# Top-k mask of an attention kernel: one parametric relu on ScalarE in place of a relu and a GpSimd subtraction

## The chip, the cores and the metric

The kernel runs on one core of a Trainium2 chip. The metric is the device time of one execution in microseconds (us); lower is better. The engines are named as in the profile: PE is TensorE's matmul (PEld its weight load), DVE is VectorE, ACT is ScalarE, POOL is GpSimd, SP is SyncE, which issues nearly all DMAs.

## The reference

Attention over 4 batches and 8 heads, 576 positions and 64 columns per head. Of each row of scores only the 32 largest stay, and the softmax runs over these. Two expert layers of 2304 x 512 x 2048 follow.

```python
scores = scale * np.matmul(q, k.transpose(0, 1, 3, 2))        # scale = 1 / 8
kth = np.partition(scores, -top_k, axis=-1)[..., -top_k:-top_k + 1]   # top_k = 32
scores = np.where(scores >= kth, scores, -1000000000.0)
attn = np.exp(scores - np.max(scores, axis=-1, keepdims=True))
attn = attn / (np.sum(attn, axis=-1, keepdims=True) + 1e-09)
x = np.matmul(attn, v)                       # then [tokens, 512]
h = np.maximum(x @ w_in, 0.0);  x = h * h @ w_out             # first layer
h = x @ w_in;  out = np.maximum(0.01 * h, h) @ w_out          # second layer
```

## The kernel before

The work of attention goes in 144 tiles of 128 rows of scores (128 x 576, fp32), two to a pair, 72 pairs. Products are exact to fp32 by splitting each operand into a high and a low part, which is why so many subtractions stand in the code.

**Scores** (L279, L280): TensorE writes a tile in two halves of 288, and ScalarE copies them into a score buffer `s` (six buffers, `NS`). The tiles of two batches are computed early, stored to HBM and loaded again when they are due (L283, L287).

**Top-k** (L834, L836): VectorE finds the 32 largest of each row in four rounds of MAX8 with a MATCH_REPLACE8 between them, so seven instructions a tile. They go into `m8`: element 0 is the row's maximum, element 31 the 32nd largest.

**Mask and exponential.** For each pair GpSimd makes two shifts by one product (`shifts`, L291): nb = -0.125 x maximum, kf = 2^100 x 32nd largest. For each tile, `drop` has ScalarE compute relu(kf - 2^100 s) (L298), which is 0 for scores that stay and huge for the others, and GpSimd subtract that from the score (L299). `expo_sum` (L303) takes exp(0.125 e + nb) on ScalarE and sums the row. GpSimd adds 1e-9 to the pair's sums (L307) and VectorE takes the reciprocal `rc` (L308). The tile `e` has four buffers.

**Behind it** TensorE transposes e (L317, L330), ScalarE copies it out (L325, or L322 with VectorE's low part L323 for later units), TensorE multiplies with V (L401, or L412). In the first units the reciprocals are transposed as well (L351), copied to `rb` (L366) and multiplied in by VectorE (`xn`, L432), and ScalarE makes the high part `xh` (L433).

**Expert blocks.** Once 512, 256, 384, ... rows of x are complete, a block of that size runs both layers, 16 steps each: twelve products into `h` (L580), an activation on ScalarE and GpSimd, and products into `acc` (L623, L625). The first block reads the weights raw (L490), converts them with ScalarE and VectorE (L513 to L519), splits them on ScalarE (L523) and GpSimd (L526), and SyncE stores the result (L534, L535); later blocks load it. A step's split may stand on GpSimd only behind the latest subtraction of `drop`: that is what `behind("pool")` asks for, with the key that L299 sets.

**Order.** The code places all of this in a grid of slots, 16 to a pair (first relu at slot 14, exponentials at 16 and 17, reciprocal at 18). A scheduler then writes for each engine one fixed order, from priorities and from its own estimate of how long things take. On the chip each engine takes its instructions in that order and waits at the first whose inputs are not there.

Of the kernel before, what the change touches and what calls it, by code (L numbers as in the profile page):

```python
# [8 lines left out]
F = mybir.dt.float32  # L9
R = mybir.dt.float32r  # L10
U = mybir.dt.uint32
AF = mybir.ActivationFunctionType
OP = mybir.AluOpType
# [3 lines left out]
FAR = 2.0 ** 100  # L17
# [54 lines left out]
def topk_attention_moe_moe2_kernel(  # L72
# [12 lines left out]
    P = 128  # L85
# [8 lines left out]
    PE, ACT, DVE, POOL, SP = nc.tensor, nc.scalar, nc.vector, nc.gpsimd, nc.sync  # L94

    const = ctx.enter_context(tc.tile_pool(name="const", bufs=1))
    pool = ctx.enter_context(tc.tile_pool(name="work", bufs=2))
# [3 lines left out]
    def bank():  # L101
        return psum.tile([P, 512], F, tag="att", name="att", bufs=3)

    ident = const.tile([P, P], F, tag="ident", name="ident")
    make_identity(nc, ident)
    scales = const.tile([P, 2, 2], F, tag="scales", name="scales")
    POOL.memset(scales[:, :, 0], -0.125)
    POOL.memset(scales[:, :, 1], FAR)

    def behind(key):  # L110

        return tc.issue_after(cur[key].ins) if key in cur else ExitStack()
# [48 lines left out]
    for i in range(4):  # L161
        x = const if i < 2 else ahead
# [124 lines left out]
        SP.dma_start(t["s"], t["sd"])  # L287

    def shifts(pr):
        t = pool.tile([P, 2, 2], F, tag="kf", name="kf", bufs=2)  # L290
        POOL.tensor_tensor(t, pr["m8"][:, :, 0:32:31], scales, op=OP.mult)  # L291
        pr["nb"], pr["kf"] = t[:, :, 0], t[:, :, 1]

    def drop(pr, i):
        t = pr["t"][i]
        t["e"] = ebufs[t["i"] % NE]
        e, x = t["e"], t["s"]
        ACT.activation(e, x, AF.Relu, bias=pr["kf"][:, i:i + 1], scale=-FAR)  # L298
        cur["pool"] = POOL.tensor_tensor(e, x, e, op=OP.subtract)  # L299

    def expo_sum(pr, i):
        e = pr["t"][i]["e"]
        ACT.activation(e, e, AF.Exp, bias=pr["nb"][:, i:i + 1], scale=0.125,  # L303
                       accum_out=pr["sum"][:, i:i + 1])

    def recip(pr):
# [68 lines left out]
    cur = dict(fill=0, rate=0.0)  # L375
# [99 lines left out]
    def w_alloc(i):  # L475
        wi = pool.tile([P, 2, 512], R, tag="wi", name="wi", bufs=3)
        wo = pool.tile([P, 2, 512], R, tag="wo", name="wo", bufs=4)
        wt[i] = (wi, wo)
        return wi, wo
# [16 lines left out]
    def w_convert(i):  # L496
        g = w_convert_steps(i)
        while True:
            with tc.high_priority(offset=CONVP):
                if next(g, 1):  # L500
                    return
            yield

    def w_convert_steps(i):
        if i >= len(steps) or not fresh[i]:
            return
        w2 = w_alloc(i)
        for raw, w in zip(wraw.pop(i), w2):
            if W64:
                lo, hi = raw[:, :, 0], raw[:, :, 1]  # L510
                b = pool.tile([P, 512], U, tag="wc", name="wc", bufs=WCB)
                v = bank()
                ACT.activation(b, lo, AF.Copy, scale=L_SCALE, bias=L_BIAS)  # L513
                ACT.activation(v, hi.bitcast(F), AF.Copy, scale=H_SCALE)  # L514
                yield 0
                vu, c = v.bitcast(U), b.bitcast(F)
                with behind("dve"):
                    DVE.scalar_tensor_tensor(b, vu, 3, b, op0=OP.logical_shift_left, op1=OP.bitwise_or)
                DVE.scalar_tensor_tensor(b, vu, 0x80000000, b, op0=OP.bitwise_and, op1=OP.bitwise_or)  # L519
                yield 0  # L520
            else:
                c = raw
            ACT.activation(w[:, 0, :], c, AF.Copy)  # L523
            yield 0
            with behind("pool"):
                POOL.tensor_tensor(w[:, 1, :], c, w.bitcast(F)[:, 0, :], op=OP.subtract)  # L526
            yield 0

    def w_store(i):
# [129 lines left out]
    for uh in uhs:  # L659
        b, hp, i = uh["b"], uh["hp"], uh.get("di")  # L660
# [79 lines left out]
    for p in range(NPAIRS):  # L740
        pr = dict(t=tiles[2 * p:2 * p + 2], p=p)
        pairs.append(pr)
        z = 16 * p
        for i, t in enumerate(pr["t"]):
            if direct(t["uh"]):
                at(z - DLEAD + 5 * i, scores, t, 0)
                at(z - DLEAD + 2 + 5 * i, scores, t, 1)
            else:
                at(z - LEAD + i, load_s, t)
            if i == 0:  # L750
                at(z + 14, shifts, pr)
            at(z + 14 + i, drop, pr, i)
            at(z + 16 + i, expo_sum, pr, i)
            if split(t["uh"]):
                at(z + 20 + i, norm, pr, i)
            at(max(z + 20 + 3 * i, z + 21 + i), pt_main, t)
        at(z + 18, recip, pr)
        at(z + 26, pt_left, pr)
# [60 lines left out]
    while slot <= last:  # L819
        p, i = divmod(slot, 16)  # L820
        if slot >= 0 and p < NPAIRS:
            pr = pairs[p]
# [6 lines left out]
            x = i % 2  # L829
            t = pr["t"][x]  # L830
            m8 = pr["m8"]
# [78 lines left out]
```

## Time and profile before

| | |
|---|---|
| three runs | 1211.27, 1215.92, 1216.74 us; median 1215.92 |
| profiled execution, span | 1212.2 us (first to last instruction; its time as a run is not one of the three) |
| PE / PEld busy | 1139.7 us (94%) / 994.3 us (82%) |
| DVE busy | 945.4 us (78%) |
| ACT busy | 877.0 us (72%) |
| POOL busy | 791.0 us (65%) |

The table is an average over stages with different limits, and an instruction's busy time overlaps the start of the next, so two instructions in a row take a little less than twice the mean. "Idle before" in a group of instructions is time in which the engine stood still just before them, with what ended it. The chain of waits follows the end of the execution back, at each step to what released it.

### The profile page before, as it was taken

The page shows a single profiled execution, that of the slowest core. Times are in us where ns is not written, and L with a number is a line of the kernel's source. Part 1 is how long each engine was busy: PE and PEld are TensorE (multiplying, and loading weights), DVE is VectorE, ACT ScalarE, POOL GpSimd, SP SyncE. Part 2 cuts the span into 40 slices and gives each one's busy share as a digit, 9 for nine tenths or more (in the row PEclk, how much of TensorE's full clock was granted, in tenths as well). Part 3 has the DMA queues.
Part 4 walks back from the last instruction along what each step waited for, and adds up shares of the span by engine and source line. Part 5 has one row for each costly group of instructions (what it writes and reads, how often), then busy time and mean ns, then how long its engine had stood idle before and what let it go on. Part 6 is the DMA issues. An engine that isn't in the chain of part 4 may idle for free.

```text
span 1212.2 us, 20368 instructions
## 1 busy us (share of the span) xinstructions
PE 1139.7 (94%) x6388; PEld 994.3 (82%) x6388; DVE 945.4 (78%) x1944; ACT 877.0 (72%) x1939; POOL 791.0 (65%) x948
## 2 busy tenths in 40 slices
PE   5898878998899999999999999999999999999998
PEld 4676766886677879988998898788788899999997
DVE  7999999668888899999999999999999910110122
ACT  6889899888899997877767777676777763334322
POOL 7998977877889886667777685666576754004300
PEclk9899997999999999999999999999999999999999
DMA  9665656879889888889988788667576579779974
GB/s 308 230 226 194 196 196 245 268 252 315 306 292 343 296 279 272 301 289 367 349 294 286 256 280 285 202 229 233 193 232 223 197 261 374 255 254 339 359 251 137
DMA packets 110521, 323.24 MB, mean 267 GB/s; under 512 B 17488, under 2 KB 25680, under 8 KB 110416
## 3 DMA queue, kind: packets, MB, share of 16 engines
q1 hardware_dynamic: 107776, 317.24, 77.1%
q10 hardware_dynamic: 2640, 4.72, 1.1%
q8 instruction: 51, 0.84, 0.3%
q14 instruction: 54, 0.44, 0.1%
HBM read 254.54 MB, written 67.37 MB: 266 GB/s over the span
## 4 chain that ended last, share of the span: by engine, by line
PE 67%; ACT 10%; DVE 9%; DMA 3%; issue 2%; POOL 1%; ACTq 0%; SPq 0%; POOLq 0%
PE h L580 28%; PE acc L623 14%; PE acc L625 13%; DVE m L834 4%; PE att L412 3%; DVE w L836 3%; PE att L317 3%; DMA wraw<-in_w_dram 2%; PE att L401 2%; ACT e L303 2%; PE att L279 1%; ACT att L514 1%; ACT stage L280 1%; DVE PTs L323 1%; ACT s L280 1%
## 5 line engine op out<-in xcount | busy, mean ns | idle before, releaser
L580 PE MATMUL h<-xh,wi 128*128 128x512 f32 (+2 forms) x1280 | 350.0, 345 | 9.1 <-ACT wi L523 3.9
L834 DVE MAX8 m<-w 128x8 f32<-128x576 f32 x432 | 312.7, 748 | 1.5
L580 PEld LDWEIGHTS h<-xh,wi 128*128 128x128 f32 x1280 | 226.8, 190 | 38.6 <-ACT wi L523 4.3
L299 POOL TENSOR_TENSOR e<-s,e 128x576 f32<-128x576 f32 x144 | 203.4, 1431 | 26.6 <-ACT e L298 25.4
L836 DVE MATCH_REPLACE8 w<-m,w 128x576 f32<-128x576 f32 x288 | 213.2, 743 | 0.5
L580 PE MATMUL h<-xl,wi 128*128 128x512 f32 (+2 forms) x640 | 206.5, 340 | 1.4 <-DVE xl L637 1.1
L606 POOL TENSOR_TENSOR gl<-ga,gh 128x512 fp32r<-128x512 f32 (+2 forms) x160 | 162.8, 1017 | 38.1 <-ACT gh L605 32.5
L623 PE MATMUL acc<-gh,wo 128*128 128x512 f32 (+2 forms) x768 | 155.1, 340 | 0.0
L625 PE MATMUL acc<-wo,gh 128*128 128x512 f32 x576 | 151.5, 398 | 3.0 <-ACT gh L605 3.0
L603 POOL TENSOR_TENSOR ga<-ga,gb 128x512 f32<-128x512 f32 (+2 forms) x80 | 81.3, 1017 | 107.6 <-ACT gb L602 105.4
L623 PEld LDWEIGHTS acc<-gh,wo 128*128 128x128 f32 x768 | 125.9, 188 | 10.8 <-ACT gh L591 0.4
L580 PEld LDWEIGHTS h<-xl,wi 128*128 128x128 f32 x640 | 120.4, 189 | 14.7 <-DVE xl L637 4.0
L303 ACT ACTIVATE e<-e,kf 128x576 f32<-128x576 f32 x144 | 112.5, 782 | 17.3 <-POOL e L299 17.0
L625 PEld LDWEIGHTS acc<-wo,gh 128*128 128x128 f32 x576 | 103.9, 188 | 23.2 <-ACT gh L605 4.7
L298 ACT ACTIVATE e<-s,kf 128x576 f32<-128x576 f32 x144 | 105.7, 778 | 22.4 <-POOL kf L291 20.3
L834 DVE MAX8 m<-s 128x8 f32<-128x576 f32 x144 | 104.7, 748 | 13.4 <-ACT s L280 12.4
L592 POOL TENSOR_TENSOR ga<-ga 128x512 f32<-128x512 f32 (+2 forms) x80 | 66.2, 828 | 68.2 <-ACT gh L591 66.0
L836 DVE MATCH_REPLACE8 w<-m,s 128x576 f32<-128x576 f32 x144 | 107.0, 743 | 0.6
L317 PE MATMUL att<-ident,e 128*128 128x128 f32 x576 | 89.4, 284 | 13.0 <-ACT e L303 7.5
L312 ACT ACTIVATE e<-e,rc 128x576 f32<-128x576 f32 x108 | 78.0, 773 | 21.3 <-DVE rc L308 21.1
L317 PEld LDWEIGHTS att<-ident,e 128*128 128x128 f32 x576 | 69.8, 145 | 26.6 <-ACT e L303 12.8
L623 PE MATMUL acc<-gl,wo 128*128 128x512 f32 (+2 forms) x384 | 86.7, 345 | 0.2 <-POOL gl L606 0.2
(96 smaller groups left out, 2174.4 us busy)
## 6 DMA issues: line engine op xcount, KB each, us to landing
wi<-wd SPq DMA_DIRECT2D x160, 512.0 KB, 5.1
wo<-wd SPq DMA_DIRECT2D x160, 512.0 KB, 5.3
wraw<-in_w_dram SPq DMA_DIRECT2D x64, 512.0 KB, 5.6
sd<-stage SPq DMA_DIRECT2D x72, 288.0 KB, 2.8
s<-sd SPq DMA_DIRECT2D x72, 288.0 KB, 4.8
wd<-wi SPq DMA_DIRECT2D x32, 512.0 KB, 6.0
wd<-wo SPq DMA_DIRECT2D x32, 512.0 KB, 6.2
kraw<-in_k_dram SPq DMA_DIRECT2D x16, 576.0 KB, 4.3
```

The source lines that it names most:

```text
L298: ACT.activation(e, x, AF.Relu, bias=pr["kf"][:, i:i + 1], scale=-FAR)
L299: cur["pool"] = POOL.tensor_tensor(e, x, e, op=OP.subtract)
L303: ACT.activation(e, e, AF.Exp, bias=pr["nb"][:, i:i + 1], scale=0.125, accum_out=pr["sum"][:, i:i + 1])
L312: ACT.activation(e, e, AF.Copy, scale=pr["rc"][:, i:i + 1])
L317: PE.transpose(ps[:, j * P:(j + 1) * P], t["e"][:, j * P:(j + 1) * P], ident)
L580: PE.matmul(h[:, 0:n], lhsT=wi[:, w, c * P:(c + 1) * P], rhs=x[c][y][:, 0:n], start=cnt == 0, stop=cnt == 3 * NK - 1)
L603: POOL.tensor_tensor(a[:, 0:n], a[:, 0:n], b[:, 0:n], op=OP.subtract)
L606: (DVE if j >= GLD else POOL).tensor_tensor(gl[:, 0:n], a[:, 0:n], gh.bitcast(F)[:, 0:n], op=OP.subtract)
L623: PE.matmul(acc[c][:, 0:n], lhsT=wo[:, w, cs], rhs=g[:, 0:n], start=first, stop=last)
L625: PE.matmul(acc[c], lhsT=g[:, cs], rhs=wo[:, w, :], start=first, stop=last)
L834: cur["dve"] = DVE.max(out=m8[:, x, 8 * r:8 * r + 8], in_=t["s"] if r == 0 else t["w"])
L836: cur["dve"] = DVE.match_replace(out=t["w"], in_to_replace=m8[:, x, 8 * r:8 * r + 8], in_values=t["s"] if r == 0 else t["w"], imm_value=NEG)
```

## The change

The relu and the subtraction of `drop` become one parametric relu on ScalarE: with x = 32nd largest - s, it passes x where x is positive (the score is to be dropped) and multiplies x by 0.125 x 2^-100 where it is not. The exponential then scales by -2^100: a dropped score gives exp of a huge negative number, 0, and a kept one exp(0.125 (s - 32nd largest) + nb). The shift nb is now 0.125 x (32nd largest - maximum), made by two GpSimd instructions, and kf is gone: the parametric relu reads the 32nd largest from `m8`. The constant tile `scales` goes, and the weights' split has no `behind("pool")` any more, since nothing sets that key.

```diff
@@ kernel
-    scales = const.tile([P, 2, 2], F, tag="scales", name="scales")
-    POOL.memset(scales[:, :, 0], -0.125)
-    POOL.memset(scales[:, :, 1], FAR)
@@ shifts, drop, expo_sum
     def shifts(pr):
-        t = pool.tile([P, 2, 2], F, tag="kf", name="kf", bufs=2)
-        POOL.tensor_tensor(t, pr["m8"][:, :, 0:32:31], scales, op=OP.mult)
-        pr["nb"], pr["kf"] = t[:, :, 0], t[:, :, 1]
+        t = pool.tile([P, 2], F, tag="nb", name="nb", bufs=2)
+        POOL.tensor_tensor(t, pr["m8"][:, :, 31], pr["m8"][:, :, 0], op=OP.subtract)
+        POOL.tensor_scalar(t, t, 0.125, 1.0, op0=OP.mult, op1=OP.mult)
+        pr["nb"] = t
 
     def drop(pr, i):
         t = pr["t"][i]
         t["e"] = ebufs[t["i"] % NE]
-        e, x = t["e"], t["s"]
-        ACT.activation(e, x, AF.Relu, bias=pr["kf"][:, i:i + 1], scale=-FAR)
-        cur["pool"] = POOL.tensor_tensor(e, x, e, op=OP.subtract)
+        ACT.activation(t["e"], t["s"], AF.Prelu, bias=pr["m8"][:, i, 31:32], scale=-1.0, alpha=0.125 / FAR)
 
     def expo_sum(pr, i):
         e = pr["t"][i]["e"]
-        ACT.activation(e, e, AF.Exp, bias=pr["nb"][:, i:i + 1], scale=0.125,
+        ACT.activation(e, e, AF.Exp, bias=pr["nb"][:, i:i + 1], scale=-FAR,
                        accum_out=pr["sum"][:, i:i + 1])
@@ w_convert_steps
-            with behind("pool"):
-                POOL.tensor_tensor(w[:, 1, :], c, w.bitcast(F)[:, 0, :], op=OP.subtract)
+            POOL.tensor_tensor(w[:, 1, :], c, w.bitcast(F)[:, 0, :], op=OP.subtract)
```

Lines behind `drop` are numbered 4 lower in the changed kernel, those behind `w_convert_steps` 5 lower. The instructions of TensorE, ScalarE, VectorE and SyncE are as many as before; GpSimd has 144 fewer subtractions, 72 more small ones and two fills less. But the scheduler wrote a new order for every engine. VectorE where the first block's last x is made (a number behind m names a pair's top-k: 2556 and 2842 before are two neighbouring pairs, as 2536 and 2821 are now; xn is the product that completes x, in L432 and L428), before:

```order
L834 MAX m_2556<-w 128x8
L836 MATCH_REPLACE w<-m_2842,w 128x576
L308 RECIPROCAL rc<-sum 128x2
L836 MATCH_REPLACE w<-m_2842,s_105 128x576
L834 MAX m_2842<-w 128x8 x2
L836 MATCH_REPLACE w<-m_2842,w 128x576
L432 TENSOR_TENSOR xn<-att,rb 128x256
```

The same place in the changed kernel:

```order
L304 RECIPROCAL rc<-sum 128x2
L831 MATCH_REPLACE w<-m_2536,w 128x576 x2
L829 MAX m_2536<-w 128x8 x2
L831 MATCH_REPLACE w<-m_2536,w 128x576
L428 TENSOR_TENSOR xn<-att,rb 128x256
L831 MATCH_REPLACE w<-m_2821,s_101 128x576
```

Before, xn stood in the middle of the second pair's rounds; now it stands ahead of the second pair's first replace, with a last MAX8 of the first pair still behind it. Counted from the start of the program, 149 MAX8 and 112 MATCH_REPLACE8 stood ahead of it, and 145 and 108 do now.

ScalarE at the same place (the masks and exponentials of the pair that is then under way; xh is the first block's last copy), before:

```order
L298 ACTIVATE e_112<-s_108,kf 128x576
L298 ACTIVATE e_113<-s_109,kf 128x576
L280 ACTIVATE s_106<-att 128x288
L366 ACTIVATE rb<-att 64x256
L514 ACTIVATE att<-wraw 128x512
L303 ACTIVATE e_112,sum<-e_112,kf 128x576
L280 ACTIVATE s_106<-att 128x288
L433 ACTIVATE xh_658<-xn 128x256
```

And in the changed kernel:

```order
L295 ACTIVATE e_109<-s_105,m_2536 128x576
L277 ACTIVATE s_103<-att 128x288
L429 ACTIVATE xh_652<-xn 128x256
L510 ACTIVATE att<-wraw 128x512
L321 ACTIVATE PT<-att 128x4x128
L510 ACTIVATE att<-wraw 128x512
L295 ACTIVATE e_110<-s_106,m_2536 128x576
L299 ACTIVATE e_109,sum<-e_109,nb 128x576
```

The second mask and the first exponential of that pair have moved from ahead of xh to behind it, and the masks read m directly.

VectorE at the 48th of the 72 reciprocals, in the stage of the later units, before:

```order
L340 TENSOR_TENSOR PTs<-att,PTs 64x256
L834 MAX m_8747<-w 128x8
L834 MAX m_8890<-w 128x8
L836 MATCH_REPLACE w<-m_8747,w 128x576
L308 RECIPROCAL rc<-sum 128x2
L836 MATCH_REPLACE w<-m_8890,w 128x576
L418 TENSOR_TENSOR xf<-att,tmp 64x256
```

And in the changed kernel, where m_8696 and m_8838 are the same two pairs:

```order
L336 TENSOR_TENSOR PTs<-att,PTs 64x256
L829 MAX m_8838<-s_103 128x8
L829 MAX m_8838<-s_104 128x8
L831 MATCH_REPLACE w<-m_8696,w 128x576
L829 MAX m_8696<-w 128x8
L304 RECIPROCAL rc<-sum 128x2
L829 MAX m_8696<-w 128x8
```

The reciprocal has moved ahead of rounds that it stood behind: 394 MAX8 of the program came before it, and 391 do now. Of eleven reciprocals looked at, each fourth from the 28th to the 68th, nine stand behind one to three MAX8 fewer than before, two behind as many.

## Rows read from the trace of the kernel before

**Rows 1.** Busy time of each engine in four stretches; columns as in the first line.

```profile
0.00:205.00 205.00, 163.20 (x851) 130.33 (x851) 193.71 (x413) 176.11 (x464) 175.53 (x247) 0.92 0.69 228
205.00:450.00 245.00, 232.68 (x1133) 188.75 (x1133) 202.24 (x382) 223.54 (x458) 208.60 (x208) 0.98 0.85 291
450.00:975.00 525.00, 512.26 (x2979) 455.55 (x2978) 514.73 (x1086) 392.80 (x827) 358.05 (x425) 1.00 0.78 263
975.00:1212.00 237.00, 231.52 (x1430) 219.70 (x1428) 34.74 (x66) 84.59 (x193) 48.85 (x69) 1.00 0.81 283
```

**Rows 2.** Chain of waits from 205 to 450 us, shares of that stretch.

```profile
by line: PE h L580 26.3%; PE acc L625 14.5%; DMA wraw<-in_w_dram 10.6%; PE acc L623 9.4%; PE att L401 4.0%; ACT att L514 4.0%; issue 3.3%; PE att L279 2.5%; ACT wc L513 2.4%; ACT e L303 2.2%; ACT wi L523 1.9%; ACT wo L523 1.7%; DMA wd<-wo 1
```

**Rows 3.** Groups of instructions, whole span: busy us, mean ns | idle before <-releasers.

```profile
L299 POOL TENSOR_TENSOR e<-s,e 128x576 f32<-128x576 f32 x144 | 203.4, 1431 | 26.6 <-ACT e L298 25.4 <-PE att L317 0.9
...
L303 ACT ACTIVATE e<-e,kf 128x576 f32<-128x576 f32 x144 | 112.5, 782 | 17.3 <-POOL e L299 17.0
...
L298 ACT ACTIVATE e<-s,kf 128x576 f32<-128x576 f32 x144 | 105.7, 778 | 22.4 <-POOL kf L291 20.3 <-PE att L330 1.0 <-issue 0.6
...
L291 POOL TENSOR_TENSOR kf<-m,scales 128x4 f32<-128x4 f32 x72 | 14.4, 200 | 26.7 <-DVE m L834 25.4
...
L308 DVE RECIPROCAL rc<-sum 128x2 f32<-128x2 f32 x72 | 11.1, 154 | 2.7 <-POOL sum L307 2.3
...
L116 ACT ACT_TABLE_LOAD x1 | 1.3, 1283 | 0.7 <-PEq L897 0.7
```

**Rows 4.** Pieces of the chain of waits, 185 to 206: start us, us, what.

```profile
194.16 0.99 POOL e L299
...
195.53 1.42 POOL e L299
196.95 1.23 POOL wi L526
198.18 1.25 POOL wo L526
...
200.46 0.20 POOL kf L291
...
200.69 1.44 ACT e L298 x2
...
202.45 0.38 ACT rb L366
...
205.04 1.22 PE h L580 x2
```

**Rows 5.** GpSimd's busy time in line L299 by stretch (the first number after the comma).

```profile
205.00:450.00 245.00, 28.42 (x20) 0.98 0.85 291
450.00:975.00 525.00, 123.91 (x88) 1.00 0.78 263
```

**Rows 6.** VectorE's later MAX8, from 100 to 200 and from 900 to 975 us.

```profile
L834 DVE MAX8 m<-w 128x8 f32<-128x576 f32 x57 | 40.6, 745 | 0.0
...
L834 DVE MAX8 m<-w 128x8 f32<-128x576 f32 x36 | 25.8, 746 | 0.1
```

**Rows 7.** VectorE's instructions in order of time around xn: start us, us.

```profile
201.32 1.41 DVE L834 MAX8 m<-w 128x8 f32<-128x576 f32 x2
202.65 0.07 DVE L836 MATCH_VALUE_LOAD w<-m,w 128x8 f32 x1
...
203.37 0.41 DVE L432 TENSOR_TENSOR xn<-att,rb 128x256 f32<-128x256 f32 x1
```

**Rows 8.** SyncE's queue waiting, 205 to 450 us: total us, times, longest.

```profile
SPq L490 <- ACT att L514: 83.9, 42, 8.1
SPq L534 <- POOL wi L526: 26.4, 19, 3.7
SPq L535 <- POOL wo L526: 25.5, 16, 4.7
```

**Rows 9.** VectorE waiting, 205 to 450 us, in the same columns.

```profile
DVE wc L518 <- ACT att L514: 24.2, 15, 3.6
```

## Prediction

> **What bounds the kernel now.** I read the span first in four stages [rows 1], cut where TensorE starts the first expert block (205), where VectorE's load changes (450) and where the top-k work ends (975). In each stage the reader is to see which engine has no room. Up to 205 it is VectorE: 193.7 of 205 us busy, the rest mostly start-up. From 450 to 975 it is VectorE again, 514.7 of 525, beside a TensorE that is almost as full (512.3). In the last stage only TensorE matters, 231.5 of 237. The stage from 205 to 450 is mixed: TensorE 232.7, ScalarE 223.5, GpSimd 208.6 and VectorE 202.2 of 245. Here the weights are read raw, split and stored, and the chain of waits carries 10.6% of this stage as landing time of raw weights [rows 2].
>
> So GpSimd, which the change relieves, is nowhere the fullest engine. Its subtraction costs 144 x 1.431 = 206 us when each is taken by itself, 203.4 as busy time [rows 3], and yet ScalarE waited for it only 17.0 us in all. What it is worth must be read from the chain. The chain of waits shows it on the path at one place that counts, just ahead of the first expert block [rows 4]: two subtractions of 0.99 and 1.42 us, behind them two weight splits (1.23 and 1.25), which by the code may not be issued before the subtraction, and then the shift kf, for which ScalarE's relus wait while the copy rb, on which the block hangs, is queued behind them.
>
> **The change part by part.** The sum is made against this execution's span, 1212.2 us; the median of the runs, 1215.9, is 3.7 above it, and I add that at the end.
>
> *The subtraction goes.* 144 x 1.43 us leave GpSimd: 28.4 of its load in the mixed stage (20 of them) and 123.9 from 450 to 975 [rows 5], the rest up to 205. From 450 to 975 this is hidden already: VectorE never stops there, and its top-k rounds don't wait for the masked scores. Worth there: 0.
>
> *Does VectorE run faster with a quieter GpSimd?* From 100 to 200 us a MAX8 took 745 ns, from 900 to 975, where GpSimd does much less, 746 [rows 6]; no effect, so 0. The Trainium skill (GPSIMD Engine Reference, Specifications) says that GpSimd shares its memory interface with VectorE and that they contend when a VectorE instruction has two SBUF inputs or runs in a two-port mode. By that rule the VectorE-bound stages could get shorter; by the rows the MAX8, more than half of the top-k work, does not feel it, and the sum stays.
>
> *The shift.* One product of 200 ns for kf and nb [rows 3] becomes two small instructions for nb. The second, on 128x2, has that 200 ns as its nearest row: 72 x 0.2 = 14.4 us more GpSimd time. It lies beside the two parametric relus of the pair (1.44 us for two relus now [rows 4]), since these no longer wait for the shift but for VectorE's last MAX8 itself. The cover is gone when GpSimd's queue is more than a microsecond late; then the exponential waits for nb as the relu waited for kf before (20.3 us in all [rows 3]), with ScalarE's copies queued behind.
>
> *Prelu for Relu.* The same 128x576 elements with one per-partition operand, on the same engine. Nearest rows: Relu 778, Exp 782 ns [rows 3]. I take 778, cost 0; at 782 it would be 0.6 us over all 144, so the ends are 0 and +0.6 and no gain. The table is another matter. The program of before loads one activation table, 1283 ns [rows 3]; in the changed ScalarE order there is still one load, at its head. The Trainium skill (ScalarE: Activation LUTs, Table sets) says that functions come in sets and that each switch costs about 2.7 us; by that, an Exp and a Prelu from different sets would be a loss of hundreds of microseconds. The order shows no switch, so the sum carries none.
>
> *The order around the first block (term A).* The product xn closes the last head pair of the first expert block; TensorE's block starts 1.7 us behind it (203.37 [rows 7], 205.04 [rows 4]). In the old VectorE order 149 MAX8 and 112 replaces stand ahead of it, in the new one 145 and 108: four rounds less. Two MAX8 take 201.32 to 202.65, one replace with its load 202.65 to 203.37 [rows 7], so this is 4 x 0.665 + 4 x 0.72 = 5.5 us of VectorE time. VectorE has been late for nothing there, so its order is its clock. ScalarE is the next that could be late: ahead of the same block's copy xh it has one relu and one exponential less, about 0.78 + 0.78 = 1.6 us [rows 3], plus its waits for GpSimd. The true gain lies between 1.6 and 5.5; I take 4.5, nearer to VectorE, because VectorE is the fuller of the two up to 205 (193.7 against 176.1 [rows 1]). The four rounds are not saved, only done later: in the mixed stage, where VectorE has 43 us free.
>
> *The mixed stage (term B).* SyncE stood 26.4 + 25.5 = 51.9 us waiting for GpSimd's weight splits before it could store them [rows 8], and the next raw loads are issued behind on the same queue. The splits may now go ahead of the softmax work, and 28.4 of GpSimd's 208.6 us are gone, 13.6%. If SyncE's waits shrink by as much, that is 7.1 us; but raw loads are only a tenth of this stage's chain, ScalarE is 91% busy with unchanged work and VectorE's longest wait is for ScalarE (24.2 us [rows 9]), not for GpSimd. Bounds 0 and 7; I take 2.5, a third. What is late next is ScalarE.
>
> *The rest.* The constant tile and its two fills go, at the start, beside the first loads: 0. Score buffers are released one GpSimd instruction earlier, so reloads of scores leave earlier on SyncE; no engine of the path waits for these: 0. The last stage is the same products in the same order: 0.
>
> Sum: 1212.2 - 4.5 - 2.5 = 1205.2, plus 3.7: **1209 us**.
>
> **The rivals.**
>
> *Rival 1, nothing arrives.* The scheduler wrote an order that assumes early softmax results; if ScalarE, not VectorE, sets the pace up to 205, A is only 1.6, and the mixed stage, which depends on ScalarE and on raw weights, gives it back. For it: ScalarE's load is unchanged, and GpSimd is on the chain almost nowhere else. Against it: xn came in its VectorE place without delay. It gives 1212 to 1219, about 1216.
>
> *Rival 2, more.* If the raw loads really hang on SyncE's waits for GpSimd, half of their 10.6% of 245 us on the chain may go: 13 us, with A in full 18.5: 1193.7 + 3.7, some 1197. For it: 51.9 us of SyncE waiting. Against it: before its raw loads it waits longest for ScalarE, 83.9 us [rows 8]. The port rule above would also come out near here; the MAX8 rows speak against it.
>
> *Rival 3, slower: the reciprocal blocks VectorE.* In the new order each reciprocal stands earlier among the top-k rounds. Of the 44 pairs after 450 us one has on average 1 to 2 MAX8 and as many replaces less ahead of it, some 2 us. VectorE takes its instructions in order, so when sum or nb is late, all top-k rounds behind the reciprocal stop, in the stage where VectorE is the bound. Now that costs 2.3 us over all 72 [rows 3]. At 0.5 us a pair it would be 44 x 0.5 = 22: 1212.2 - 4.5 + 22 + 3.7 = 1233. It decides from 0.1 us a pair (4.5 / 44). Against it: the chain from relu to exponential loses a subtraction of 1.43 us and more, about what the reciprocal was moved.
>
> *Rival 4, the table.* Should the functions need separate sets, even one load of 1.283 us a pair and back, 144 in all, is 185 us: about 1400. The order excludes it but for an error of mine.
>
> **How the numbers follow.** A measurement of this kernel can tell about 0.5%, so faster means below 1209.8 and slower above 1222.0. The forecast has 0.48, with its own range 1204 to 1214, of which 0.29 falls below 1209.8 and 0.19 within; rival 1 has 0.22, all within; rival 2 0.16, all faster; rival 3 0.12 and rival 4 0.02, slower. Together faster 0.45, same 0.41, slower 0.14. The range takes the forecast, rival 1 and the upper half of rival 2, 1196 to 1222, and leaves out rival 3, rival 4 and the lower half of rival 2, 0.22.
>
> **What would show it.** A: the first expert product of the full run starts near 200 instead of 205, and the first stage's four rounds turn up as VectorE time after it. B: SyncE's waits for the weight splits fall well under 52 us and the stage from the first block to VectorE's full load is 2 to 3 us shorter than 245. Prelu: a mean within a few ns of 778, one table load. Rival 3: waits of the reciprocal for the sum well over 2.3 us. VectorE's stage of 525 us should keep its length. I am wrong in kind if GpSimd is still on the chain ahead of the first block, or if VectorE's busy share after 450 falls.

## The result and the profile after

The changed kernel takes 1221.74 us (median of 5 runs), the kernel before beside it 1213.13: a ratio of 1.0063, 95% interval [1.0043, 1.0083], so slower by 0.6%. (Ratios are worked out from all runs of both kernels, so they need not be those of the medians.) The forecast was 1209, a gain of 7 us. The profiled execution of after has a span of 1221.0 us against 1212.2.

The windows of after, cut as those of [rows 1]:

```profile
0.00:205.00 205.00, 160.39 (x845) 128.44 (x845) 185.69 (x397) 172.19 (x456) 128.73 (x225) 0.92 0.69 227
205.00:450.00 245.00, 228.15 (x1109) 184.13 (x1108) 204.68 (x391) 223.86 (x458) 181.20 (x194) 0.99 0.84 286
450.00:975.00 525.00, 511.91 (x2963) 458.15 (x2962) 513.15 (x1079) 385.28 (x818) 244.06 (x383) 0.98 0.78 264
975.00:1221.00 246.00, 240.17 (x1477) 226.64 (x1475) 42.00 (x80) 92.42 (x209) 51.42 (x73) 1.00 0.80 277
```

Behind each stretch and its length stand the busy times of TensorE, its weight loads, VectorE, ScalarE and GpSimd, then the granted clock. GpSimd has lost what was to go, 791.0 us before and 605.4 now in all. VectorE, the third, is the one to look at: by 205 us it has worked 185.69 instead of 193.71, 8.0 us less, and it gets only part of that back in the stage behind. It ends its top-k work later, with 42.00 us instead of 34.74 still to do behind 975, and the last stage, where TensorE is the full engine, is 9 us longer.

The groups of after that answer to [rows 3]:

```profile
L295 ACT ACTIVATE e<-s,m 128x576 f32<-128x576 f32 x144 | 112.0, 779 | 13.7 <-DVE m L829 10.2
L299 ACT ACTIVATE e<-e,nb 128x576 f32<-128x576 f32 x144 | 111.1, 775 | 5.5 <-POOL nb L289 5.4
L304 DVE RECIPROCAL rc<-sum 128x2 f32<-128x2 f32 x72 | 10.9, 152 | 4.8 <-POOL sum L303 4.5
L113 ACT ACT_TABLE_LOAD x1 | 1.3, 1283 | 0.7 <-PEq L892 0.7
```

The parametric relu lasts 779 ns, the relu before 778; there is one table load; the exponential waits 5.4 us in all for its shift, where it waited 17.0 for the subtraction and the relu 20.3 for kf. The instructions cost what was forecast. The loss is in waits.

VectorE's waits of after up to 205 us (line waiting, line waited for, total us, times, longest):

```profile
DVE m L829 <- ACT e L295: 5.6, 4, 4.0
DVE xn L428 <- PE att L397: 4.7, 1, 4.7
DVE q L255 <- ACT q L113: 4.5, 1, 4.5
```

The same of before:

```profile
DVE q L258 <- ACT q L116: 4.5, 1, 4.5
DVE m L834 <- ACT s L280: 1.9, 2, 1.3
DVE xn L432 <- ACT rb L366: 0.9, 1, 0.9
```

The first row of after is new: MAX8 waits for the parametric relu. The longest of the four in the timeline of after (start, duration, idle time before in brackets), VectorE and, around it, ScalarE:

```profile
135.65 0.83 ACT L295 ACTIVATE e<-s,m 128x576 f32<-128x576 f32 x1
...
141.00 0.71 ACT L277 ACTIVATE stage<-sp 128x288 f32<-128x288 f32 x2 [3.33 <-DMA sd<-stage]
141.59 0.78 ACT L295 ACTIVATE e<-s,m 128x576 f32<-128x576 f32 x1
...
142.47 0.76 DVE L829 MAX8 m<-s 128x8 f32<-128x576 f32 x1 [4.01 <-ACT e L295]
```

ScalarE stands 3.33 us at a copy whose buffer is still being stored. The pair's second relu is queued behind. It reads the kth value from m8, of which there are two, so the next MAX8 that needs that buffer starts 0.1 us after the relu's end and 4 us late. Before, GpSimd's product took the kth value out of m8 into kf in 0.2 us, and m8 came free without ScalarE, as long as ScalarE was not so late that both buffers of kf were still in use. I call this **the hold**.

The second row is as long, and it isn't the hold: at 89 us, ahead of the first MAX8 that waits for a relu (119.48), VectorE stands 4.71 us at an xn for TensorE's product. There too ScalarE had just stood for a buffer that was being stored, 2.45 us, with the copies for that product queued behind. ScalarE's copies into the stage (tile `stage`, where scores lie until they are stored), before (first) and after:

```profile
L280 ACT ACTIVATE stage<-sp 128x288 f32<-128x288 f32 x144 | 55.1, 433 | 8.5 <-PE sp L279 4.3 <-issue 3.1 <-PE sd L279 0.5
```

```profile
L277 ACT ACTIVATE stage<-sp 128x288 f32<-128x288 f32 x144 | 53.1, 437 | 16.2 <-DMA sd<-stage 7.4 <-PE sp L276 6.2 <-issue 1.9
```

The 7.4 us of waiting for stores are new as well.

Where the lateness becomes time: the windows from 755 to 790 us of before (first) and after.

```profile
755.00:790.00 35.00, 33.36 (x159) 27.56 (x158) 34.70 (x75) 23.42 (x45) 21.58 (x23) 0.97 0.67 219
```

```profile
755.00:790.00 35.00, 27.37 (x119) 22.40 (x120) 34.17 (x71) 22.65 (x43) 11.12 (x16) 0.85 0.61 196
```

TensorE works 6.0 us less here. Its next instruction is a transpose of softmax results, and the normalisation ahead of it on ScalarE is late:

```profile
760.57 1.97 PE L313 MATMUL att<-ident,e 128*128 128x128 f32 x8 [5.59 <-ACT e L308]
```

After this stand its granted clock is 0.50 of full speed, the lower level of 1.2 GHz, from 760 to 764 us; the mean over the window is 0.85, and was 0.97 before. From 790 us on TensorE is the bound: it is busy 424.55 of the 431.0 us that are left, against 415.38 of 422.0 before.

### The profile page after: what moved, and what is told of

The parts are those of the page before. It is cut to its first block, busy times and chain, and to the rows that moved or that the text cites. A ratio compares the mean times of both kernels' runs of the same rounds, so it can differ in the third digit from the quotient of the medians.

```text
span 1221.0 us, 20215 instructions
## 1 busy us (share of the span) xinstructions
PE 1140.6 (93%) x6388; PEld 997.4 (82%) x6388; DVE 945.5 (77%) x1944; ACT 873.7 (72%) x1939; POOL 605.4 (50%) x874
## 4 chain that ended last, share of the span: by engine, by line
PE 58%; DVE 4%; ACT 1%; issue 0%; ACTq 0%
PE h L575 25%; PE acc L620 13%; PE acc L618 12%; PE att L408 4%; PE att L313 3%; DVE m L829 1%; DVE w L831 1%; PE att L326 1%; PE att L276 1%; DVE PTs L319 0%; DVE xl L632 0%; ACT e L295 0%; ACT xh L631 0%; DVE xf L414 0%; DVE PTs L336 0%
## 5 line engine op out<-in xcount | busy, mean ns | idle before, releaser
L618 PE MATMUL acc<-gh,wo 128*128 128x512 f32 (+2 forms) x768 | 156.4, 342 | 0.1
L295 ACT ACTIVATE e<-s,m 128x576 f32<-128x576 f32 x144 | 112.0, 779 | 13.7 <-DVE m L829 10.2
L299 ACT ACTIVATE e<-e,nb 128x576 f32<-128x576 f32 x144 | 111.1, 775 | 5.5 <-POOL nb L289 5.4
L600 ACT ACTIVATE gh<-ga 128x384 fp32r<-128x384 f32 (+2 forms) x112 | 58.8, 525 | 38.3 <-POOL ga L598 28.4
L620 PE MATMUL acc<-wo,gl 128*128 128x512 f32 x288 | 83.9, 398 | 0.0
```

Of the source, the lines that this page charges most:

```text
L295: ACT.activation(t["e"], t["s"], AF.Prelu, bias=pr["m8"][:, i, 31:32], scale=-1.0, alpha=0.125 / FAR)
L600: ACT.activation(gh[:, 0:n], a[:, 0:n], AF.Copy)
L618: PE.matmul(acc[c][:, 0:n], lhsT=wo[:, w, cs], rhs=g[:, 0:n], start=first, stop=last)
L620: PE.matmul(acc[c], lhsT=g[:, cs], rhs=wo[:, w, :], start=first, stop=last)
```

## The experiments

The change does two things to a reader of the diff, and a third that the diff doesn't show: it swaps instructions, it lets ScalarE hold m8, and it makes the scheduler write another order. To take these apart, most runs below hold the order with a list: at the end of the program's text, each instruction of an engine gets an edge to its predecessor in the wanted order, one that fixes the issue order and waits for nothing.

```diff
     assert len(ready) == len(blocks)
+    for eng, text in ORDER.items():
+        rank = _array.array("H", _zlib.decompress(_base64.b64decode(text)))
+        ...
+        for a, b in zip(rank, rank[1:]):
+            tc.add_manual_dep(have[b], have[a].name, mybir.DependencyInfo(
+                mybir.DependencyClass.NoSync, mybir.DependencyReason.DATA), reason="order")
```

The line numbers of such kernels are some 17 to 21 higher. All ratios are against the kernel before, run beside each on the same chip (its medians there were 1213 to 1216 us). "Idle" is VectorE's idle time in the first 950 us of the profiled execution, 950 less its busy time by the windows. This column and the span are of one execution each, which in e11, e13 and e14 took 2 to 5 us longer than the kernel's median.

| run | instructions | order | m8 | median us | ratio, 95% | idle | span |
|---|---|---|---|---|---|---|---|
| before | old | before | 2 | 1213.13 | 1 | 60.1 | 1212.2 |
| after | new | its own | 2 | 1221.74 | 1.0063 [1.0043, 1.0083] | 71.1 | 1221.0 |
| e1 | new | before | 2 | 1233.74 | 1.0143 [1.012, 1.0167] | 78.4 | 1231.6 |
| e2 | old | after, in part | 2 | 1328.96 | 1.0944 [1.0921, 1.0968] | 156.4 | 1323.5 |
| e3 | new | scheduler's | 3 | 1231.72 | 1.0134 [1.0116, 1.0152] | 76.7 | 1228.1 |
| e4 | new + product | scheduler's | 2 | 1218.06 | 1.0022 [1.0007, 1.0036] | 64.0 | 1215.2 |
| e5 | new | after | 3 | 1219.25 | 1.0033 [1.0017, 1.0049] | 69.3 | 1219.2 |
| e6 | new | before | 3 | 1212.92 | 0.9986 [0.9974, 0.9998] | 58.3 | 1211.0 |
| e7 | new, kth copied | before | 2 | 1215.58 | 1.0009 [1.0, 1.0018] | 59.7 | 1214.2 |
| e8 | new | e4 | 3 | 1213.32 | 0.9994 [0.9981, 1.0006] | 58.8 | 1209.7 |
| e9 | new | after, reciprocals later | 3 | 1229.82 | 1.0127 [1.0107, 1.0147] | 77.7 | 1228.8 |
| e10 | new | before, reciprocals earlier | 3 | 1215.03 | 1.0009 [0.9996, 1.0021] | 62.0 | 1214.2 |
| e11 | new + product | e4 | 3 | 1218.2 | 1.0027 [1.0014, 1.0041] | 66.9 | 1218.5 |
| e12 | new | e4 | 2 | 1214.25 | 0.9981 [0.9968, 0.9994] | 60.4 | 1210.9 |
| e13 | new + product | before | 3 | 1218.12 | 1.0026 [1.0013, 1.0039] | 65.2 | 1219.9 |
| e14 | old | before, by a list | 2 | 1216.26 | 1.0005 [0.9989, 1.002] | 65.8 | 1219.3 |
| e15 | old, shift of two | before | 2 | 1217.4 | 1.002 [1.0008, 1.0032] | 60.6 | 1213.3 |

One thing shows down the last two columns: span less idle is 1150 to 1155 us in every row but e2. So, to within these 5 us, what VectorE stands ahead of 950 us comes back as time of the kernel.

### Does the loss come with the order or with the instructions? (e1, e2)

```diff
+ORDER = {"DVE": ..., "Activation": ..., "PE": ..., "SP": ..., "Pool": ...}
```

e1 is the changed kernel's text with before's order, e2 before's text with after's order on VectorE, TensorE and SyncE.

> The changed kernel's instructions, held on every engine in the order in which the kernel before has them (on GpSimd with the two shift operations where the one product stood and without the 144 subtractions). Theory 'order' (the loss is in what the new order queues ahead of what on VectorE and ScalarE, not in the new operations): as long as before or shorter, 1208 to 1215 us; VectorE's idle time by 205 us falls from 19.3 back to about 11 us. Theory 'hold' (the parametric relu on ScalarE reads the kth value out of m8, so a pair's m8, of which there are two, comes free later than when GpSimd copied it away early, and MAX8 waits): the hold is still there, so 1218 to 1223 us, and the waits of MAX8 on the relu in the first stage (5.6 us after) stay.

> The mirror of e1: the kernel before's instructions, with VectorE, TensorE and SyncE held in the order of the changed kernel; ScalarE and GpSimd, whose lists can't be the same with the subtraction between relu and exponential, are left to the scheduler. Theory 'order': 1218 to 1224 us, as the changed kernel, or more, since the exponential now also waits for GpSimd. Theory 'hold': 1211 to 1216 us, as before, since nothing is held longer.

e1 is not as before but 1.4% slower, over twice the loss of after, and above both expectations. Its waits on VectorE up to 205 us:

```profile
DVE m L846 <- ACT e L312: 13.3, 9, 2.3
DVE q L272 <- ACT q L130: 5.5, 1, 5.5
DVE m L846 <- ACT s L294: 1.3, 1, 1.3
```

The theory 'order' falls: before's order doesn't bring before's time back. 'Hold' is right in kind and too small: in the old order it is 13.3 us instead of 5.6. The scheduler makes its order from the same buffers and waits, and after's own order has less of it. After 450 us the hold goes on under other names, as this piece of e1's timeline shows, where the MAX8 whose wait is put down to "issue" starts as the two relus of 673.25 end (673.25 + 1.48):

```profile
673.25 1.48 ACT L312 ACTIVATE e<-s,m 128x576 f32<-128x576 f32 x2
...
674.81 1.42 DVE L846 MAX8 m<-s 128x8 f32<-128x576 f32 x2 [1.50 <-issue]
```

e2 went far outside both theories, for a reason that neither held (waits up to 1000 us):

```profile
DVE rc L321 <- POOL sum L320: 85.7, 45, 5.9
```

After's order has the reciprocals earlier on VectorE. With the subtraction still in the chain the sums aren't there, and VectorE stands 85.7 us in 45 waits. That is rival 3 of the prediction, in a kernel in which it happens. (After itself waits 4.5 us for sums, before 2.3.)

### The hold by itself (e3, e5, e6, e7)

```diff
-                pr["m8"] = pool.tile([P, 2, 32], F, tag="m8", name="m8", bufs=2)
+                pr["m8"] = pool.tile([P, 2, 32], F, tag="m8", name="m8", bufs=3)
```

That is e3, with the order left to the scheduler; e5 with the order of after held, e6 with that of before. e7 keeps two buffers and copies:

```diff
+        k = pool.tile([P, 2], F, tag="kf", name="kf", bufs=2)
+        POOL.tensor_scalar(k, pr["m8"][:, :, 31], 1.0, 1.0, op0=OP.mult, op1=OP.mult)
+        pr["kth"] = k
...
-        ACT.activation(t["e"], t["s"], AF.Prelu, bias=pr["m8"][:, i, 31:32], ...
+        ACT.activation(t["e"], t["s"], AF.Prelu, bias=pr["kth"][:, i:i + 1], ...
```

> The changed kernel with three buffers of m8 instead of two; the scheduler then makes a third order. Theory 'hold': the waits of MAX8 on the parametric relu (5.6 us in the first stage) go, and the time comes down to 1212 to 1216 us. Theory 'order': those waits go too, but the time is that of yet another order, 1216 to 1224 us, and VectorE's idle time by 205 us stays above 15 us.

> The changed kernel with a third buffer of m8, and this time all five engines held in the changed kernel's own order, so that the buffer is the only difference (in e3 the scheduler had made another order). Theory 'hold': MAX8 no longer waits for the parametric relu (5.6 us in the first stage of the changed kernel, perhaps some us more later), part of which the stage of weight conversion had absorbed, so 1213 to 1219 us. Theory 'misfit' (what costs is the order itself, made for times that the chip doesn't keep, and the waits of MAX8 are only where it shows): the waits turn into others and it stays at 1219 to 1224 us.

> e1 (the new operations in the order of before) with a third buffer of m8 and nothing else. Theory 'hold': e1's waits of MAX8 on the relu (13.3 us by 205 us, and some 8 us after 450 us that the wait list puts down to other engines but that end with the relu) go, VectorE's idle time by 950 us falls from 78 to about 60 us, and the time to 1211 to 1217 us. Theory 'misfit': 1226 to 1234 us.

> e1 with two buffers of m8 as it has, but the kth values copied into a small tile of their own by one short operation of GpSimd behind the shift, and the parametric relu reads them there: m8 is then let go by GpSimd, as in the kernel before. Theory 'hold': the same gain as e6, 1211 to 1218 us, since it is the tile that the relu keeps that counts. Theory 'misfit': 1226 to 1234 us. If e6 gains and this does not, it is something else that a third m8 frees.

In the order of before, the third buffer takes e1's 1.0143 to 0.9986, 19 us, and the copy on GpSimd to 1.0009, 16 us. Both take away only what the relu holds, so in that order the hold is shown as the whole loss. VectorE's waits of e6 up to 205 us have no relu left:

```profile
DVE q L272 <- ACT q L130: 4.3, 1, 4.3
DVE KT L255 <- ACT KT L130: 1.3, 1, 1.3
DVE m L846 <- ACT s L294: 1.2, 1, 1.2
```

In the order of after, the third buffer takes 1.0063 to 1.0033 (e5), 3.6 us of the 7.6; with the two intervals the difference is 0.30% give or take 0.26. The other 4 us stay, with no relu in VectorE's waits: that part lies in the order. At 1219.25 us it lies where the two expectations meet (up to 1219, from 1219). Nor is all of the 3.6 us shown to be the hold: in the two traces the xn at 89.19 us in after comes at 86.29 in e5, 2.9 us earlier, ahead of any MAX8 that was held. e3, which 'hold' wanted at 1212 to 1216 us and 'order' at 1216 to 1224, missed both and shows how much an order can cost: the same instructions and buffers as e5 and e6, but the scheduler's third order, 1.0134, 1.5% over e6. The relu's waits did shrink, to 2.6 us by 205 us. There VectorE waits for scores being loaded, a row that neither e5 nor e6 has (e3, 205 to 950 us):

```profile
DVE m L829 <- DMA s<-sd: 11.9, 11, 2.2
```

### What the removed subtraction is worth (e4, e8, e11, e13)

```diff
         ACT.activation(t["e"], t["s"], AF.Prelu, bias=pr["m8"][:, i, 31:32], scale=-1.0, alpha=0.125 / FAR)
+        cur["pool"] = POOL.tensor_tensor(t["e"], t["e"], ones576, op=OP.mult)
```

The product by ones takes 1432 ns (e13), the subtraction took 1431, and stands in its place. With it come the tile of ones and, as in before, the `behind("pool")` of the weights' splits. e4 leaves the order to the scheduler; e11 holds e4's order with three m8; e13 holds before's order with three m8. e8 and e6 are their partners without the product.

> The changed kernel with 144 operations of GpSimd put back between the parametric relu and the exponential, 128x576 with two inputs as the removed subtraction was, here a product of the tile with ones that changes no value (some 1431 ns each on GpSimd, 206 us in all). Theory 'order': the scheduler goes back to an order near that of before, 1211 to 1217 us, though the kernel does more work than the changed one. Theory 'hold': the relu still reads m8 as late as in the changed kernel, so 1218 us or more. A third theory, that the removed work on GpSimd has no part in the time at all and any reordering costs as much: 1213 to 1224 us, without relation to either.

> A candidate: the changed kernel's operations (without the subtraction or the product that stood for it in e4) in the order that the scheduler had made for e4, with three buffers of m8. Theory 'hold': the order was worth 1218 us with the hold in it, without it and without GpSimd's 206 us 1208 to 1215 us. Theory 'misfit': an order made for other operations costs, as in e1 and e2, 1222 us or more.

> What GpSimd's relief and the shorter chain are worth by themselves: e8 (three m8, the order of e4) with the 144 products by ones of GpSimd put back between relu and exponential, as in e4, in that same order. It does all that the kernel before does on GpSimd and e8 does not. Theory 'relief counts' (the gain that was forecast is there but hidden): 1216 to 1220 us, 3 to 7 us over e8. Theory 'nothing arrives': 1213 to 1216 us, within 2 us of e8, since VectorE, which sets the time, waited for nothing that GpSimd was late with.

> The pair of e8 and e11 once more, in the order of before: e6 (the new operations, three m8, 1212.92 us) with the 144 products by ones of GpSimd put back where the subtraction stood. It asks what the subtraction's removal is worth at an order that does not change. Theory 'relief counts everywhere': 1216 to 1219 us, 4 to 5 us over e6 as e11 over e8; then the parametric relu in place of relu would cost the kernel about what the removal gives, as before itself is at 1214 us. Theory 'it depends on the order': in an order that was made with the subtraction in it GpSimd is late for nobody, 1212 to 1215 us.

e4, which does more work than the changed kernel, is faster than it: 1.0022 against 1.0063. By itself it decides little, as its order is another one and 1218.06 us lies in the ranges of two of its three theories, 1 us above that of 'order'. At an order that doesn't change, the product costs 1.0027 against 0.9994 (e11, e8), 4.0 us, and 1.0026 against 0.9986 (e13, e6), 4.9 us. Each difference is uncertain by some 2 us, by the two intervals. So "relief counts everywhere" holds, and the removal is worth 4 to 5 us. The exponential shows the way it acts, first e13, then e6:

```profile
L319 ACT ACTIVATE e<-e,nb 128x576 f32<-128x576 f32 x144 | 112.2, 780 | 22.9 <-POOL e L315 22.5
```

```profile
L316 ACT ACTIVATE e<-e,nb 128x576 f32<-128x576 f32 x144 | 112.0, 779 | 0.2
```

22.5 us of ScalarE standing go, and 7 us of VectorE's idle time behind it (65.2 to 58.3, in an execution of e13 that was 3.5 us above its median).

### Where is the rest of after's order? (e9, e10)

VectorE waits 9.1 us for sums in e5 and 0.8 in e6, so I moved the reciprocals on VectorE alone, 68 of them later in e5 (e9) and 56 earlier in e6 (e10). In VectorE's list of e9, at each of them (in e10 the other way round):

```diff
 -RECIPROCAL rc
 MAX8 or MATCH_REPLACE8, one or two
+RECIPROCAL rc
```

> e5 (the changed kernel in its own order, three m8) with 68 of the 72 reciprocals moved on VectorE behind the next one or two MAX8 or MATCH_REPLACE (1.8 on average, some 1.3 us), all else in the same order. Theory 'reciprocals': what is left of the loss in e5 (VectorE's idle time by 950 us 69.3 us against 58.3 in e6) is the 9.2 us that VectorE stands behind reciprocals whose sums are not there yet; most of it goes, and the time comes to 1213 to 1216 us. Rival 'other places': the waits move to other instructions, idle time stays above 66 us, and 1218 to 1221 us.

> The counterpart: e6 (the new operations in the order of before, three m8) with 56 of the 72 reciprocals moved on VectorE ahead of the one or two MAX8 or MATCH_REPLACE that stand before them (1.4 on average, some 1.0 us). Theory 'reciprocals': waits for the sums appear, 4 to 8 us, and the time rises to 1215 to 1220 us. Rival 'other places': the sums are there 1 us earlier too, as ScalarE no longer waits for GpSimd between the relu and the exponential, and it stays at 1212 to 1214 us, or gains as the normalisations come earlier.

e9 missed by more than the whole loss: not 1213 to 1216 but 1229.82. VectorE's waits for sums fell, to 5.2 us, but ScalarE's normalisation, which reads the reciprocal, now stands 43.4 us; first e5, then e9:

```profile
L325 ACT ACTIVATE e<-e,rc 128x576 f32<-128x576 f32 x108 | 77.7, 768 | 3.2 <-DVE rc L321 3.1
```

```profile
L325 ACT ACTIVATE e<-e,rc 128x576 f32<-128x576 f32 x108 | 78.0, 770 | 43.7 <-DVE rc L321 43.4
```

Everything queued behind it on ScalarE comes late, and VectorE with it: its wait for ScalarE's weight copies goes from 31.7 to 36.8 us (35.2 of these from 205 to 450), its waits at xn from 1.3 to 4.8. (By itself that row tells no loss: it is 21.1 us in before and 16.2 in e6.) e10 waits 6.1 us for sums, as expected, and costs 1.0009 against 0.9986, 2.8 us, the lower edge of it. A reciprocal has a place, set by its sum on one side and by the normalisation's place in ScalarE's order on the other; a microsecond off cost to either side, 2.8 us in e10 and 11 in e9, where ScalarE is the one that stops. So the 4 us left in e5 can't be put down to the reciprocals, or to any one place. What differs from e6 beside them: ScalarE's copies into the stage wait 3.5 us for a store to free the buffer (7.4 in after, 0.6 in e6, none before). Over all traces these waits for a store are 3.5 to 12.0 us in after, e2, e3, e5 and e9 and at most 1.9 us in the twelve others, so they go with the orders that lose (after, e5 and e9 have one order of ScalarE and SyncE); no run has a further stage buffer, which would tell whether they are a cause. The split of the 4 us stays open.

### Only the order changed (e12)

Against e8:

```diff
-                pr["m8"] = pool.tile([P, 2, 32], F, tag="m8", name="m8", bufs=3)
+                pr["m8"] = pool.tile([P, 2, 32], F, tag="m8", name="m8", bufs=2)
```

> e8 (the new operations in the order of e4) with two buffers of m8 instead of three: the changed kernel itself, with nothing but another order. Theory 'an order made for the hold': e4's order came from the scheduler with two m8 in its books, so it keeps MAX8 and the relu apart by itself, as e4 and e11 show (1218.06 and 1218.2 us with two and three); 1212 to 1216 us, no loss against before, and the changed kernel's loss is a matter of its order alone. Theory 'the hold costs in every order': some 3 us in the changed kernel's order, 21 in that of before, so here 3 to 20 us over e8, 1216 to 1233 us.

This is the changed kernel, instruction for instruction and buffer for buffer, in e4's order: 0.9981 [0.9968, 0.9994], where its own order gives 1.0063. It is faster than before, by 0.2%, and than after, by 0.8% (10 us). The hold is still there and costs nothing that shows: the whole row of it in e12, 0 to 950 us, is

```profile
DVE m L846 <- ACT e L312: 0.8, 2, 0.5
```

So the changed kernel's loss is its order. e12, e6 and e8 are the versions to keep; their intervals overlap, and e8's reaches 1.

### The control, and what the second short operation costs (e14, e15)

The edit of e15, in the kernel before with e14's list:

```diff
+        POOL.tensor_scalar(t[:, :, 0], t[:, :, 0], 1.0, 1.0, op0=OP.mult, op1=OP.mult)
         pr["nb"], pr["kf"] = t[:, :, 0], t[:, :, 1]
```

e14 is the kernel before with a list that holds its own order.

> A control: the kernel before, with its own order on all five engines held by the same written-out lists as in e1, e6 and e13. If the lists themselves cost nothing, it is the kernel before: 0.998 to 1.002 of it. If e13's 1.0026 comes from the lists (other semaphores, other buffers chosen), it stands at 1.002 to 1.004, and all runs with lists have to be read against this one.

> e14 with a second short operation of GpSimd behind the product of the shift, a product by one on the pair's first column (128x2, some 200 ns, 72 of them), as the changed kernel's shift has two. It asks whether the 0.26% that e13 stands above before, with the same work on GpSimd, is the second operation: kf, for which both relus wait, comes 0.2 us later in every pair. Theory 'second operation': 1.002 to 1.004 of before. Theory 'not it': within 0.1% of e14, and the cause stays with the relu's later reading of the scores' maximum, or stays open.

The list costs nothing that shows, 1.0005 [0.9989, 1.002]; its one profiled execution was a long one (span 1219.3). e15 gives 1.002 [1.0008, 1.0032]. It is over before, but its interval overlaps e14's: inconclusive. Why e13, with the work of before in the order of before, is 0.26% over it, therefore stays open; the second short operation may be a part, as e15, with as many GpSimd operations in the same order as e13, stands at 1.0020 beside its 1.0026.

## Why the prediction was wrong

**What failed first is a line that isn't there.** The part on "Prelu for Relu" costs the instruction by its duration and is right to the nanosecond (779 against 778); "The rest" goes through the score buffers that come free earlier. Neither asks which buffer comes free later. The relu's bias moved from kf, which GpSimd had made, to m8, which VectorE needs again. That made four waits and 5.6 us in after's first stage, and at most 3.6 us of the 7.6 us loss (e5, 0.30% give or take 0.26). No rival named it.

**Term A failed at one sentence:** "VectorE has been late for nothing there, so its order is its clock." The four rounds, 5.5 us, did move behind xn. But VectorE lost 8.0 us in the stage that it had not lost before, and -5.5 + 8.0 gives +2.5: xn came at 205.34 instead of 203.37 [rows 7], the product behind it at 207.35 instead of 205.04 [rows 4]. (That is the block's first product with the last part of x; three others of the block run earlier, at 190.09 before and 185.68 after.) The forecast was "near 200". An order says what is ahead of what; the engine keeps that pace only if what it waits for moved too. Two waits come to more than the 8.0: the MAX8's 4.01 us at 142 us and the xn's 4.71 at 89, where all waits at xn took 1.3 before. ScalarE, the "next that could be late", was the one: ahead of both it stood for a stage buffer, 3.33 and 2.45 us, and VectorE behind it. At the xn the clock counted too: TensorE worked 0.05 us from 79 to 81 us, its granted clock was then 0.50 (1.2 GHz) from 83 to 86, and ten products of L397 took 4.21 us that took 2.62 in e5, at 1.00. In e5, the same order with a third m8, xn came at 199.70 and the product at 201.70, 3.3 us earlier than before: there term A arrived in the main, and the loss lies behind it.

**Term B failed in the changed kernel and holds in size elsewhere.** SyncE's waits for the weight splits should have fallen from 51.9 us [rows 8]. From 205 to 450 us in after:

```profile
SPq L486 <- ACT att L510: 75.0, 39, 5.2
SPq L529 <- POOL wi L521: 46.1, 24, 5.2
SPq L530 <- POOL wo L521: 25.0, 21, 3.4
```

They rose to 71.1, though GpSimd has 27 us less to do in the stage (208.6 to 181.2): the splits themselves end later, the 61st of the 64 at 432.0 instead of 427.9 us, and SyncE stands in front of them. In e6, with the order held, they fall to 18.5 + 24.6 = 43.1, 8.8 us less; the 7.1 of the prediction was about right. But VectorE's work in the stage grows only from 202.24 to 203.48, 1.2 us, of the 2.5 that were taken. What was named as next is what holds it: VectorE's wait for ScalarE's weight copies [rows 9] is 24.4 us there.

**The worth of the subtraction was about right in size and in place, and for another reason.** 7.0 us were forecast, 4 to 5 are there at an unchanged order. Much of it is there ahead of the first block, where term A had it: the product behind the last xn comes at 207.02 us in e13 and 202.19 in e6, at 207.13 in e11 and 202.19 in e8, while the spans of these executions differ by 8.9 and 8.8. But no round has moved in these pairs; ScalarE's exponential no longer stands for GpSimd. For the stage from 450 on the prediction has "Worth there: 0." That stands: VectorE's busy time from 450 to 950 us is 492.09 in e13 and 492.91 in e6, to 205 us 191.88 and 195.30.

**No faster VectorE: right.** MAX8 takes 748 ns with GpSimd's 806 us (e13) and 750 with its 608 (e6), against 748 before. The Trainium skill (GPSIMD Engine Reference, Specifications) has VectorE and GpSimd contend where VectorE reads two SBUF inputs or runs in a two-port mode; MAX8 has one input, and its rows show nothing of this. VectorE's busy time as a whole is 945.8 us in e13 and 944.3 in e6, so no more than 1.5 of the 4 to 5 us can lie there.

**Rival 3 was right as a mechanism and wrong in size here.** Sums cost after 4.5 us, not 22; in e2, with the subtraction left in, 85.7. **Rival 1** is nearest to what the change is worth as a whole: with the hold removed and the order of before, 0.9986, 1.7 us, since what the removal gives is mostly spent by e13's open 0.26%. The cause that decided, another order of the scheduler, was in the sum only as a gain; as a loss it stood in rivals 1 and 3, neither of them with the waits that came.

## What to carry to other kernels

When an operand moves from a copy to the original, ask who writes the original next, how many buffers there are and how far the new reader's queue can fall behind: a reader on a busy in-order engine holds the writer, and the cost shows on the writer (MAX8's 4.01 us here). When a scheduler makes the order, a change of instructions and a change of order come together; hold the order with a list and run both halves, since here the instructions in an order that suits them gained 0.1 to 0.2% (e6, e12) and the orders alone ranged over 1.5% (e6, e3). Don't mend one wait by shifting one instruction on one engine: its reader on the other engine has a place too (e9).
